# One VectorE step per decoded weight, PSUM as four two-bank tiles, and the later batches' attention form from batch 1 on

## The chip, the core and the metric

The kernel runs on one core of a Trainium2 chip. A core has a matrix engine (TensorE, PE in the profile; PEld is its weight loading), three engines that work on vectors (VectorE or DVE, ScalarE or ACT, GpSimd or POOL), and SyncE (SP), which here issues every DMA. Matrix products land in PSUM, eight banks of 512 fp32 columns on each of 128 partitions; everything else lies in SBUF or DRAM. The engines run side by side, each in its own program order, and wait for one another by semaphores that a framework places: it follows which instructions touch which tile. The metric is the device time of one execution in microseconds.

## The reference

Attention with two kinds of window over 8 batches, 8 heads, 576 positions and 64 channels, then a two-layer network on its output, whose nonlinearity is a rational function:

```python
scores = scale * np.matmul(q, k.transpose(0, 1, 3, 2))
scores = np.where(masks[None, :, :, :], scores, -1000000000.0)   # 32 last positions, or every 4th of 128
attn = np.exp(scores - max) / (sum + 1e-09)
x = np.matmul(attn, v)                                           # 4608 tokens x 512
h = x @ w_in                                                     # 512 x 2048
g = (a[0] + a[1]*h + a[2]*h2 + a[3]*h3) / (1 + |b[0]|*|h| + |b[1]|*h2 + 1e-6)
out = g @ w_out                                                  # 2048 x 512
```

The weights arrive as 64-bit floats.

## The kernel before

**Two halves of work.** The attention is cut into 48 units, six for each batch (class `Unit`, line 258): one unit is the scores of 128 rows against their windows, softmax, and the product with v. The network is cut into 144 tiles (class `Tile`, line 711): nine chunks of 512 tokens (eight batches' first 512, and one chunk `x_left` of what is left over from all batches) by 16 blocks of 128 hidden channels. One tile is 12 matmuls into `h` (line 720), the rational function on ACT, POOL and DVE (lines 773 to 788), and 12 matmuls into the four accumulators `out0` to `out3` (line 755). Every operand of the network is split into a high and a low part, so each product is three matmuls. Chunk 0's tiles run in two groups of eight with all of chunk 1 between them, and chunks 2 to 8 follow (line 943).

**The order.** A planner (class `Plan`, line 78) knows every step with its engines and an assumed duration, plays the program through, and writes the instructions down in the order in which its steps start; each engine keeps that order (`pin`). Its tables (`DUE`, `LATE`, `SLACK`, lines 31 to 34) shift the ranks of steps, and `takes` says which buffer a step needs and whose end frees it. The planner doesn't wait on the chip: it only sets the order.

**PSUM.** Two banks `h` take turns (`PS_BUFS`, line 848), four hold the accumulators, and two, `att` and `dec`, serve the attention and the decode. Each is a tile of its own until batch 3's attention starts; then `att` and `dec` become the two halves of one two-bank tile, `pair` (lines 851 to 864). From then on the halves are used by the later batches' units and, at the very end, by two tiles of the network, whose `h` goes into `att` and `dec` (line 717).

**The uses of `h`.** For each tile PE writes it with 12 matmuls; ACT reads it twice (`a<-h`, the absolute value, and `t<-h,na_t`, a line of the numerator); DVE then has `t<-t,h`, `h<-t,na_t,h`, `h<-h,na_t,r` and `a<-a,h`. Between DVE's second and third step lies a longer way by other buffers: ACT and POOL make the denominator in `a` and `r`, and ACT takes its logarithm and the exponential of the negative.

**Attention, two forms.** Batches 0 to 2 use one bank for scores, with places in halves of 64 rows; masks are added by PE in most units (`ON_PE`, line 29), and then the exponents go block by block, six instructions with their sums (`exp_bank`, line 346). PE transposes the probabilities (line 381 on), two copies put them into a zeroed tile, and PE multiplies them with v (`o_ps`). Batches 3 to 7 (`rows`) use both halves of `pair` at once in blocks of 32 rows; DVE transposes the probabilities in 32 x 32 blocks, they go to DRAM and come back in another order, PE multiplies, DVE transposes the result and it takes a second trip through DRAM. One unit is open at a time: the product with v of a unit is issued with the next one's scores (line 169).

**Decode.** A weight tile of 128 x 512 64-bit floats is fetched as words (32 such tiles, `w_fetch`), scaled by ACT (`w_scale`, from the high word), and put together by three DVE steps through the bank `dec`: shift left by 3, or in the low word's top bits, or in the sign (lines 653 to 663). A copy makes the high part (ACT or POOL) and POOL's subtraction the low part (lines 669 to 675). Staging tiles (`stage`, four of them) are shared by the decode, the trips through DRAM, and the results.

Of the kernel before, what the change touches and what calls it, by code (L numbers as in the profile page):

```python
# [11 lines left out]
I32 = mybir.dt.int32  # L12
AF = mybir.ActivationFunctionType
# [9 lines left out]
NU = 6  # L23
SPARE = "wo6"
HALF = NF // 2
BOTH, ON_ACT, ON_DVE = {"ACT": 450, "DVE": 500}, {"ACT": 450}, {"DVE": 500}


ON_PE = [[0, 0, 1, 1, 1, 1], [1, 1, 1, 1, 1, 1], [1, 0, 1, 1, 1, 1], [0, 0, 0, 0, 0, 0], [0, 0, 0, 0, 0, 0], [0, 0, 0, 0, 0, 0], [0, 0, 0, 0, 0, 0], [0, 0, 0, 0, 0, 0]]
PLACE = [(BOTH, BOTH), (ON_ACT, ON_ACT), (ON_DVE, ON_ACT), (ON_ACT, ON_DVE), (ON_ACT, ON_DVE), (ON_ACT, ON_DVE), (ON_ACT, ON_DVE), (ON_ACT, ON_DVE)]  # L30
DUE = [(13.95, 6.95), (76.77, -0.16), (93.75, -11.62), (46.1, 1.05), (120.4, 10.64), (81.33, -3.2), (120.08, -7.86), (195.87, 20.0)]

LATE = {"ab": -20.8, "ql": -91.15, "pl": 134.92, "qq": -111.7, "t1": 37.34, "t2": -29.76, "ln": 10.32, "ex": -6.24, "g0": 1.41, "g1": -62.33, "g2": 0.04, "gh": -105.34, "gl": 53.4, "out": 3.13}
SLACK = {"sc": -0.06, "qk0": 5.5, "v0": -9.17, "load": -12.74, "wi": 2.56, "wo": 1.08, "w": -12.47, "gl": 1.36, "out": 2.98}

EARLY_TILES = 36

ROWS = 3
LEFT = S - 512
NQ, NKEY, NV = 2 * 6 * 64, 2 * 224, 3 * 2 * 2 * 64  # L40
RQ, RKEY = 4 * 3 * 32, 4 * 128
LOG_SHIFT = 40
GUARD = 1.0 + 1e-6

# [33 lines left out]
class Plan:  # L78
# [21 lines left out]

    def due(self):
# [21 lines left out]
    def run(self):  # L123
# [10 lines left out]
        while ready:  # L134
            options = []
            for o in ready:
                before = list(o.deps)
                for tag, _ in o.takes:
                    bufs, groups = self.tags[tag]
                    if len(groups) >= bufs:  # L140
                        users = groups[len(groups) - bufs]
                        if any(u.end is None for u in users):
                            break
                        before += users
                else:
                    for eng, ns in o.engs.items():
                        shared = ports if o.lock or eng == "POOL" else 0.0
                        t = max([free.get(eng, 0.0), shared] + [d.after(eng) for d in before])
                        options.append((t, o, eng, ns))
# [12 lines left out]
            if o.lock or eng == "POOL":  # L162
# [16 lines left out]
def tile_attention_moe(  # L179
# [3 lines left out]
    qk_rows: bass.AP,  # L183
# [15 lines left out]

    early_banks = ExitStack()  # L200
    apart = early_banks.enter_context(tc.tile_pool(name="psum_apart", bufs=1, space=bass.MemoryType.PSUM))


# [54 lines left out]
    class Unit:  # L258
        def __init__(self, b, u):
            self.b, self.u, self.n = b, u, b * NU + u  # L260
            self.rows = b >= ROWS

        def load_qk(self):

            n = RQ + RKEY if self.rows else NQ + NKEY
            t = att.tile([P, NQ + NKEY], F32, tag="qk", name=f"qk{self.n}")[:, :n]
            load(t, qk_rows[self.n - ROWS * NU] if self.rows else qk[self.n])
            cut = RQ if self.rows else NQ
            self.q, self.k = t[:, :cut], t[:, cut:]

        def load_q(self, pool, tag):

            self.q = pool.tile([P, NQ], F32, tag=tag, name=f"q{self.n}")
            load(self.q, qk[self.n, :, :NQ])

        def load_k(self, pool, tag):
            self.k = pool.tile([P, NKEY], F32, tag=tag, name=f"k{self.n}")
            load(self.k, qk[self.n, :, NQ:])
# [5 lines left out]
        def bank(self, tag, what):  # L284
            if tag in PAIR:
                return two_banks(tag, f"{what}{self.n}", self.rows)
            return psum.tile([P, 512], F32, tag=tag, name=f"{what}{self.n}", bufs=PS_BUFS[tag])

        def scores(self, tag, masked):
            q_t = self.q.rearrange("p (h j m) -> p h j m", h=2, j=6)  # L290
            k_t = self.k.rearrange("p (h k) -> p h k", h=2)
            self.s = ps = self.bank(tag, "s_ps")
            pairs = [(h, j) for j in range(6) for h in range(2)]

            if masked:

                for j, cnt, m in self.masks():
                    mm(ps[:, 64 * j : 64 * (j + cnt)], ident_b, m, start=(j == 0), stop=False)
            for h, j in pairs if self.b else sorted(pairs):
                cols = slice(64 * j, 64 * j + 64)  # L300
                mm(ps[64 * h : 64 * h + 64, cols], q_t[:, h, j, :], k_t[:, h, 32 * j : 32 * j + 64], start=not masked, stop=not masked or j == 5)

        def scores_rows(self):
            join_banks()
            q_t = self.q.rearrange("p (g i c) -> p g i c", g=4, i=3)
            k_t = self.k.rearrange("p (g k) -> p g k", g=4)
            for i in range(3):
                for g in range(4):
                    for r in range(2):
                        half = slice(64 * r, 64 * r + 64)  # L310
                        mm(pair[0][32 * g : 32 * g + 32, r, 64 * i : 64 * i + 64], q_t[half, g, i], k_t[half, g, 32 * i : 32 * i + 64])
# [5 lines left out]
        def mask(self):  # L317
            s = self.blocks()
            for j, cnt, m in self.masks():
                if self.rows:  # L320
                    part = s[:, j // 3 : (j + cnt) // 3]
                    m = m.rearrange("p (r i) k -> p r i k", i=3)
                else:
                    part = s[:, j : j + cnt]
                tt(part, part, m, ALU.add)

        def blocks(self):
            if self.rows:
                return pair[0][:, :, :192].rearrange("p r (i k) -> p r i k", k=64)
            return self.s[:, :384].rearrange("p (j k) -> p j k", k=64)  # L330
# [6 lines left out]
        def max(self):  # L337
            self.mx, self.mx3 = self.small("mx")
            mx = self.mx.rearrange("p (r i) -> p r i", r=2) if self.rows else self.mx
            pin(nc.vector.tensor_reduce(mx, self.blocks(), axis=AX, op=ALU.max))  # L340
# [5 lines left out]
        def exp_bank(self, pool, tag):  # L346
            self.new_p(pool, tag)
            s = self.blocks()
            self.sm, self.sm3 = self.small("sm")
            for j in range(6):  # L350
                act(self.p[:, j], s[:, j], AF.Exp, bias=self.mx3[:, j // 2, j % 2 : j % 2 + 1], scale=0.125, accum_out=self.sm[:, j : j + 1])

        def new_p(self, pool, tag):
            self.p = pool.tile([P, 6, 64], F32, tag=tag, name=f"p{self.n}", bufs=2 if pool is att else 1)

        def sub(self, pool, tag):
            self.new_p(pool, tag)
            if self.rows:
                p = self.p.rearrange("p (r i) k -> p r i k", r=2)
                mx = self.mx.rearrange("p (r i) -> p r i", r=2)  # L360
                tt(p, self.blocks(), mx.unsqueeze(3).to_broadcast([P, 2, 3, 64]), ALU.subtract)
                return
            tt(self.p, self.blocks(), self.mx.unsqueeze(2).to_broadcast([P, 6, 64]), ALU.subtract)
# [15 lines left out]
        def transposes(self, tag):  # L379
            self.t = self.bank(tag, "t_ps")  # L380
# [3 lines left out]

        def turn(self):

            self.turned = work.tile([P, 512], F32, tag="stage", name=f"u{self.n}", bufs=4)[:, :384]
# [646 lines left out]
```

## Time and profile before

| | |
|---|---|
| median of 3 runs | 919.88 us (915.46 to 919.99) |
| the profiled execution | 917.92 us |
| its span, first to last instruction | 916.1 us |
| TensorE busy | 884.9 us, 7277 matmuls |
| VectorE, ScalarE, GpSimd busy | 727.1, 687.7, 506.8 us |
| DMA | 97.11 MB, mean 106 GB/s |

The page of the profile gives busy times by engine, the chain of work that ended last, and the costliest groups of instructions. A row of the timeline has the start in us, the duration, the engine, the line, the operation with the tiles that it writes and reads, and in brackets how long its engine had stood idle and what ended that. Buffer numbers are left out of names, so `h` stands for all tiles of that name. Busy TensorE means that at least one matmul is in its pipeline; matmuls overlap there. The granted clock is the share of full speed that TensorE was allowed.

### The profile page before, as it was taken

The numbers are of one execution on the slowest core, as the hardware profiler recorded it, in microseconds if no ns is written. First come the engines' busy times: TensorE is split into PE (matmuls) and PEld (weight loads), VectorE is DVE, ScalarE is ACT, GpSimd is POOL, SyncE is SP. The second block draws the span as 40 slices with busy tenths as digits, with TensorE's granted clock in tenths as the row PEclk, the third lists the DMA queues.
The fourth block names the chain that finished last, engine by engine and source line by source line (L and its number), as shares of the span: only waits on it lengthen the run. The fifth ranks groups of instructions, "written<-read, shape, count | busy, mean of one in ns | idle before, by whom it ended". The sixth has DMA issues, their size and how long they took to land.

```text
span 916.1 us, 19423 instructions
## 1 busy us (share of the span) xinstructions
PE 884.9 (97%) x7277; PEld 718.7 (78%) x7277; DVE 727.1 (79%) x1305; ACT 687.7 (75%) x1228; POOL 506.8 (55%) x469
## 2 busy tenths in 40 slices
PE   6789989999999999999999999999999999999998
PEld 5666768877788777888888888888888888888876
DVE  5899999996778787878788878888878687567656
ACT  4889988877767777777787777777777787777774
POOL 2467677864455555556555564655455545444442
PEclk9799999999999999999999999999999999999999
DMA  9734930024434333433353334333333110001001
GB/s 331 262 119 161 390 131 1 1 90 148 127 111 140 89 124 114 142 99 110 108 165 98 120 98 155 101 118 91 117 92 104 40 47 0 1 1 47 0 1 47
DMA packets 64414, 97.11 MB, mean 106 GB/s; under 512 B 22208, under 2 KB 42304, under 8 KB 64320
## 3 DMA queue, kind: packets, MB, share of 16 engines
q1 hardware_dynamic: 64320, 95.88, 31.7%
q8 instruction: 57, 0.93, 0.4%
q14 instruction: 37, 0.30, 0.1%
HBM read 73.57 MB, written 22.28 MB: 105 GB/s over the span
## 4 chain that ended last, share of the span: by engine, by line
PE 78%; DMA 8%; DVE 6%; ACT 4%; issue 1%; SPq 1%; POOL 1%; POOLq 0%; DVEq 0%; ACTq 0%
PE out L213 36%; PE h L213 36%; DMA wi_raw<-in_w_in_dram 4%; PE pair L213 4%; DVE a L222 2%; ACT r L216 1%; SPq L210 1%; DVE h L222 1%; DMA part<-os 1%; DMA v<-in_vp_dram 1%; PE o_ps L213 1%; PE s_ps L213 1%; DMA wo_raw<-in_w_out_dram 1%; POOL a L225 1%; DMA k<-in_qk_dram 1%
## 5 line engine op out<-in xcount | busy, mean ns | idle before, releaser
L213 PE MATMUL h<-xh,wi 128*128 128x512 f32 x1136 | 378.2, 394 | 6.8 <-DVE a L222 6.7
L213 PE MATMUL out<-gh,wo 128*128 128x512 f32 x1136 | 354.4, 393 | 1.1 <-DVE os L228 1.1
L225 POOL TENSOR_TENSOR a<-r,a 128x512 f32<-128x512 f32 x141 | 182.4, 1293 | 241.2 <-ACT r L216 233.4
L213 PEld LDWEIGHTS h<-xh,wi 128*128 128x128 f32 x1136 | 214.1, 188 | 58.3 <-DVE a L222 12.0
L213 PEld LDWEIGHTS out<-gh,wo 128*128 128x128 f32 x1136 | 210.3, 188 | 45.9 <-DVE os L228 1.6
L213 PE MATMUL h<-xl,wi 128*128 128x512 f32 x568 | 222.1, 391 | 0.0
L213 PE MATMUL out<-gl,wo 128*128 128x512 f32 x568 | 221.5, 390 | 0.0
L225 POOL TENSOR_TENSOR gl<-a,gh 128x512 fp32r<-128x512 f32 x141 | 184.7, 1310 | 18.9 <-ACT gh L216 17.2
L222 DVE SCALAR_TENSOR_TENSOR a<-a,r 128x512 f32<-128x512 f32 x141 | 98.7, 700 | 114.3 <-ACT r L216 113.9
L216 ACT ACTIVATE r<-a,ln_bias 128x512 f32<-128x512 f32 x141 | 101.8, 722 | 64.7 <-POOL a L225 64.4
L216 ACT ACTIVATE a<-h 128x512 f32<-128x512 f32 x140 | 84.0, 600 | 55.4 <-PE h L213 52.5
L213 PEld LDWEIGHTS out<-gl,wo 128*128 128x128 f32 x568 | 106.6, 188 | 22.9 <-POOL gl L225 0.5
L216 ACT ACTIVATE r<-a,ab_t 128x512 f32<-128x512 f32 x141 | 114.7, 814 | 13.2 <-DVE h L222 7.3
L213 PEld LDWEIGHTS h<-xl,wi 128*128 128x128 f32 x568 | 107.2, 189 | 21.1
L216 ACT ACTIVATE t<-h,na_t 128x512 f32<-128x512 f32 x142 | 109.6, 772 | 5.1 <-PE h L213 4.4
L222 DVE SCALAR_TENSOR_TENSOR h<-t,na_t,h 128x512 f32<-128x512 f32 x142 | 107.3, 755 | 4.8
L222 DVE SCALAR_TENSOR_TENSOR h<-h,na_t,r 128x512 f32<-128x512 f32 x142 | 106.4, 749 | 5.6 <-ACT r L216 4.4
L216 ACT ACTIVATE r<-r,exp_bias 128x512 f32<-128x512 f32 x144 | 104.1, 723 | 4.4
L219 DVE TENSOR_TENSOR t<-t,h 128x512 f32<-128x512 f32 x142 | 95.6, 673 | 13.3 <-ACT t L216 13.1
L216 ACT ACTIVATE gh<-a 128x512 fp32r<-128x512 f32 x135 | 84.8, 628 | 22.6 <-PE out L213 18.1
L222 DVE SCALAR_TENSOR_TENSOR a<-a,h 128x512 f32<-128x512 f32 x140 | 96.1, 686 | 4.4
L225 POOL TENSOR_TENSOR p<-p,sm 128x384 f32<-128x384 f32 x48 | 39.9, 831 | 67.2 <-DVE sm L374 46.3
(105 smaller groups left out, 732.9 us busy)
## 6 DMA issues: line engine op xcount, KB each, us to landing
v<-in_vp_dram SPq DMA_DIRECT2D x48, 384.0 KB, 3.6
qk<-in_qk_rows_dram SPq DMA_DIRECT2D x30, 448.0 KB, 4.6
out_dram<-os SPq DMA_DIRECT2D x36, 256.0 KB, 2.3
wi_raw<-in_w_in_dram SPq DMA_DIRECT2D x16, 512.0 KB, 8.7
wo_raw<-in_w_out_dram SPq DMA_DIRECT2D x16, 512.0 KB, 8.7
qk<-in_qk_dram SPq DMA_DIRECT2D x12, 608.0 KB, 4.5
turned<-u SPq DMA_DIRECT2D x30, 192.0 KB, 2.0
results<-y SPq DMA_DIRECT2D x30, 192.0 KB, 2.1
```

The lines of the kernel that those rows point to most:

```text
L210: pin(nc.sync.dma_start(dst, src))
L213: pin(nc.tensor.matmul(o, lhs, rhs, start=start, stop=stop))
L216: pin(nc.scalar.activation(o, i, func, **kw))
L219: pin(nc.vector.tensor_tensor(o, x, y, op))
L222: pin(nc.vector.scalar_tensor_tensor(o, x, s, y, op0, op1))
L225: pin(nc.gpsimd.tensor_tensor(o, x, y, op))
```

## The change

- **Decode.** ACT scales the high word with a function that has another slope for negative numbers (`Prelu`), so that the sign comes out of the same shift. A new pass on ACT or POOL (`w_low`) turns the low word into its top bits, in place. One DVE step (`w_join`) shifts and ors, with both inputs in SBUF. The high part's copy may now also go to DVE, the low part's subtraction too. A fetch follows the join of the weight six before it.
- **Attention.** Batches 1 and 2 take the form of the later ones, with masks added on PE. Batch 0 uses blocks of 32 rows in three pairs of banks; five of its six units take one exponent for the whole block. PE transposes its probabilities into an `h` bank, and one copy brings them to SBUF. Two units are open at a time in place of one.
- **PSUM.** Four two-bank tiles, `banks`, for the whole run: accumulators in the halves of 0 and 1, `h` in the halves of 2 by turns, attention in 3 (and the last tiles' `h` there, as before).
- **Leftovers** go to DRAM, `left_dram`, and are fetched for the last chunk in four parts. There are eight staging tiles in place of four. POOL's two steps of a tile may go to DVE in the first 36 tiles. The planner's tables are new.

```diff
+KIND = [0, 0, 0, 0, 1, 0]
+EARLY_TILES, BOTH_TILES = 36, 36
+DEPTH, STAGE, AHEAD, ON_PE = 2, 8, 6, 3
...
+            self.start, self.on_pe = b == 0, b < ON_PE
+            self.pair = banks[(0, 1, 3)[u % 3] if self.start else 3]
...
+        def transposes(self):
+            self.t = h_bank()
...
+        def place(self, eng):
+            self.pT = work.tile([P, 512], F32, tag="a", name=f"pT{self.n}")[:, :384]
+            copy(eng, self.pT, self.t[:, :384])
...
-    def w_shift(key):
-
-        wb[key] = b = two_banks("dec", "%s_b%d" % key, False)
-        pin(nc.vector.tensor_scalar(b.bitcast(I32), wf[key].bitcast(I32), 3, None, ALU.logical_shift_left))
-
-    def w_low(key):
-        bits = wb[key].bitcast(I32)
-        stt(bits, w_words(key)[:, :, 0], 29, bits, ALU.logical_shift_right, ALU.bitwise_or)
-
-    def w_sign(key):
-        stt(wf[key].bitcast(I32), w_words(key)[:, :, 1], -0x80000000, wb.pop(key).bitcast(I32), ALU.bitwise_and, ALU.bitwise_or)
+        pin(nc.scalar.activation(w, w_words(key)[:, :, 1].bitcast(F32), AF.Prelu, scale=2.0**-112, alpha=-(2.0**32)))
+
+    def w_low(key, eng):
+
+        low = w_words(key)[:, :, 0]
+        if eng == "ACT":
+            act(low, low.bitcast(U32), AF.Identity, bias=low_bias, scale=LOW_SCALE)
+        else:
+            pin(nc.gpsimd.tensor_scalar(low, low.bitcast(U32), LOW_SCALE, LOW_BIAS, ALU.mult, ALU.add))
+
+    def w_join(key):
+        bits = wf[key].bitcast(I32)
+        stt(bits, bits, 3, w_words(key)[:, :, 0], ALU.logical_shift_left, ALU.bitwise_or)
...
+        if len(joined) >= AHEAD:
+            f.follows.append(joined[-AHEAD])
...
-        hi = op({"ACT": 525, "POOL": 590}, 0, lambda e: w_hi(key, e), steps[-1])
-        lo = op({"POOL": 1280}, 0, lambda e: w_lo(key, e), hi)
+        hi = op({"ACT": 525, "DVE": 400, "POOL": 590}, 0, lambda e: w_hi(key, e), steps[-1], lock=True)
+        lo = op({"DVE": 602, "POOL": 1280}, 0, lambda e: w_lo(key, e), hi, lock=True)
...
-            if self.bank in PAIR:
-                ps = two_banks(self.bank, f"h{self.i}", True)
-            else:
-                ps = psum.tile([P, 512], F32, tag=self.bank, name=f"h{self.i}", bufs=PS_BUFS[self.bank])
+            ps = h_bank() if self.bank == "h" else banks[3][:, ("att", "dec").index(self.bank)]
...
-                ops[c, o] = psum.tile([P, 512], F32, tag=f"out{o}", name=f"out{c}_{o}_{ft}")
+                ops[c, o] = banks[o // 2][:, o % 2]
...
-            both = {"DVE": 602} if tail else {"POOL": 1253}
+            both = {"DVE": 602} if tail else {"DVE": 602, "POOL": 1253} if i < BOTH_TILES else {"POOL": 1253}
...
+    left_dram = dram.tile([P, NK, 512], F32, name="left")
...
+    banks = [psum.tile([P, 2, 512], F32, tag=f"banks{n}", name=f"banks{n}") for n in range(4)]
+    h_turn = []
+
+    def h_bank():
+        h_turn.append(None)
+        return banks[2][:, len(h_turn) % 2]
...
-    x_left = const.tile([P, NK, 512], F32, name="x_left")
...
+    def fetch_left(kt):
+        lefts[kt] = t = work.tile([P, 512], F32, tag="stage", name=f"left{kt}", bufs=STAGE)
+        load(t, left_dram[:, kt])
```

More of the change, by code (lines that the diff above doesn't have):

```diff
@@ L12 @@
 I32 = mybir.dt.int32
+U32 = mybir.dt.uint32
 AF = mybir.ActivationFunctionType
@@ L99, in takes, with shares @@
         o.takes.append((tag, users))
+    @staticmethod
+    def shares(o, eng):
+        return eng == "POOL" or (eng == "DVE" and o.lock)
     def due(self):
@@ L282, in load_v, with scores @@
             load(self.v, vp[self.n])
[L284 to L295, printed above, removed]
-                for j, cnt, m in self.masks():
[L298 to L306, printed above, removed]
+        def scores(self):
+            on_pe = self.on_pe
+            if on_pe:
+                for j, cnt, m in self.masks():
+                    for r in range(j // 3, (j + cnt) // 3):
+                        mm(self.pair[:, r, :192], ident_b, m[:, 3 * r - j : 3 * r - j + 3], start=True, stop=False)
             for i in range(3):
@@ new lines, in evac_lo @@
+                either(eng, self.dst(xl, cols, d), self.src(cols), self.dst(xh, cols, d), ALU.subtract)
+            if self.start and left:
+                self.o = work.tile([P, 512], F32, tag="stage", name=f"l{self.n}", bufs=STAGE)
+                for (first, cnt), _ in left:
+                    while cnt:
+                        n = min(cnt, 96 - first % 96)
+                        copy(eng, self.left((first, n)), self.src((first, n)))
+                        first, cnt = first + n, cnt - n
@@ new lines, in left, with put_left, plan @@
+        def left(self, cols):
+            first, cnt = cols
+            return self.o[:, :384].rearrange("p (h t) -> p h t", h=2)[:, :, first : first + cnt]
+        def put_left(self):
+            for cols, d in self.pieces()[1]:
+                load(left_dram[d], self.left(cols))
+        def plan(self, by, tags):
+            b, u, start = self.b, self.u, self.start
+            s_tag, self.o_tag = (f"s{u % 3}", f"o{u % 3}") if start and u % 3 < 2 else ("att", "dec")
+            (qp, qt), (vpool, self.vt) = tags if start else ((att, "qk"), (att, "v"))
+            self.by = by
+            lq = op({"SP": 430}, 0, lambda e: self.load_qk(qp, qt), dma=(RQ + RKEY) * 512)
+            self.lv = lv = op({"SP": 430}, 0, lambda e: self.load_v(vpool, self.vt), dma=NV * 512)
+            prev, clear = None, []
+            masks = [masked, identity] if self.on_pe else []
+            if len(Unit.open) >= DEPTH:
+                prev = Unit.open.pop(0)
@@ L538, in plan @@
             no = op({"POOL": 790}, 0, lambda e: self.norm(e), rc)
-            if rows:
+            if start:
+                tr = op({"PE": 500}, 0, lambda e: self.transposes(), no, identity)
+                pl = op(BOTH, 0, lambda e: self.place(e), tr)
+                plan.takes(tr, "h", 2, [pl])
+                self.placed = [pl]
+            else:
                 tr = op({"DVE": 540}, 0, lambda e: self.turn(), no)
@@ L717, in __init__ @@
             self.bank = {-1: "att", 0: "dec"}.get(self.n, "h")
-            self.r_buf = ("stage", 4) if self.late else ("r", 1)
+            self.r_buf = ("stage", STAGE) if self.late else ("r", 1)
         def h(self):
@@ L802, in plan @@
             Tile.last_out = outs
-            plan.takes(h, self.bank, PS_BUFS[self.bank], [g2])
+            plan.takes(h, self.bank, 2 if self.bank == "h" else 1, [g2])
             if not self.late:
@@ L901, in tile_attention_moe @@
     for u in range(NU):
-        start = {
-            "banks": (f"out{u % 2}", ("out2", "att")[u % 2], ("out3", "h")[u % 2]),
-            "tiles": (
-                (wpool, f"wi{15 - u}"),
-                (wpool, f"wo{9 - u // 2}" if u % 2 == 0 else f"wi{9 - u // 2}"),
-                (wpool, f"wo{15 - u}"),
-                (work, "t") if u % 3 == 2 else (att, "p"),
-            ),
-        }
+        tags = ((wpool, f"wi{15 - u}"), (wpool, f"wo{15 - u}"))
         last, step = DUE[0]
-        Unit(0, u).plan(last - (NU - 1 - u) * step, start)
+        Unit(0, u).plan(last - (NU - 1 - u) * step, tags)
     for key in keys:
```

372 lines of the change are left out of this document (150 added, 222 removed).

## The prediction

> **What bounds the kernel now.** I read the page first, then the table of busy time by stage, the chain that ended last, the groups of instructions, and last the timeline of the end, since the change lays the kernel's PSUM out anew.
>
> ```profile
> span 916.1 us, 19423 instructions
> ...
> PE 884.9 (97%) x7277; PEld 718.7 (78%) x7277; DVE 727.1 (79%) x1305; ACT 687.7 (75%) x1228; POOL 506.8 (55%) x469
> ...
> PE 78%; DMA 8%; DVE 6%; ACT 4%; issue 1%; SPq 1%; POOL 1%; POOLq 0%; DVEq 0%; ACTq 0%
> ```
>
> ```profile
> 0.00:40.00 40.00, 25.40 (x390) 22.12 (x390) 25.68 (x65) 24.60 (x92) 14.60 (x25) 0.88 0.80 292
> 40.00:140.00 100.00, 90.11 (x590) 70.22 (x587) 92.10 (x162) 86.44 (x200) 69.83 (x63) 0.98 0.55 203
> ...
> 720.00:880.00 160.00, 160.00 (x707) 132.53 (x706) 107.36 (x158) 122.30 (x184) 77.37 (x62) 1.00 0.04 16
> ```
>
> The columns after the stretch are PE, PEld, DVE, ACT and POOL busy, granted clock, DMA share, GB/s. From 40 us on TensorE is the bound: busy 90 of 100 us up to 140 us, where VectorE is as busy (decode), and without a break at the end. The chain shows the beat:
>
> ```profile
> 740.10 2.72 PE h L213 x12
> 742.82 2.72 PE out L213 x12
> ```
>
> One tile is 12 `h` and 12 `out` matmuls, 2.72 us each way: 5.44 us, and 144 tiles make 783 us. This holds only because `h` of tile i+1 runs while DVE and ACT still work on the `h` of tile i. The timeline of an ordinary pair of tiles:
>
> ```profile
> 875.78 0.76 DVE L222 SCALAR_TENSOR_TENSOR h<-t,na_t,h 128x512 f32<-128x512 f32 x1
> ...
> 875.93 0.39 PE L213 MATMUL h<-xh,wi 128*128 128x512 f32 x1
> ...
> 878.91 0.60 ACT L216 ACTIVATE a<-h 128x512 f32<-128x512 f32 x1 [0.52 <-PE h L213]
> 879.10 0.75 DVE L222 SCALAR_TENSOR_TENSOR h<-h,na_t,r 128x512 f32<-128x512 f32 x1
> ...
> 879.41 0.78 ACT L216 ACTIVATE t<-h,na_t 128x512 f32<-128x512 f32 x1
> ```
>
> PE starts the next `h` at 875.93 in the middle of DVE's step on the last one (875.78 to 876.54), and DVE's step at 879.10 overlaps ACT's at 878.91. These are two tiles of one bank each. At the end two tiles (`att`, `dec` of line 717) sit in the two halves of the one two-bank tile `pair`, and there nothing overlaps:
>
> ```profile
> 886.66 0.76 DVE L222 SCALAR_TENSOR_TENSOR pair<-t,na_t,pair 128x512 f32<-128x512 f32 x1
> ...
> 887.47 0.50 PE L213 MATMUL pair<-xh,wi 128*128 128x512 f32 x1 [0.49 <-DVE pair L222]
> ...
> 890.52 0.60 ACT L216 ACTIVATE spare_h<-pair 128x512 f32<-128x512 f32 x1 [1.26 <-PE pair L213]
> ...
> 891.15 0.76 DVE L222 SCALAR_TENSOR_TENSOR pair<-pair,na_t,r 128x512 f32<-128x512 f32 x1 [1.10 <-ACT spare_h L216]
> ...
> 891.95 0.69 DVE L222 SCALAR_TENSOR_TENSOR a<-a,pair 128x512 f32<-128x512 f32 x1
> ...
> 892.67 0.78 ACT L216 ACTIVATE t<-pair,na_t 128x512 f32<-128x512 f32 x1 [0.70 <-DVE a L222]
> ...
> 893.48 0.69 DVE L219 TENSOR_TENSOR t<-t,pair 128x512 f32<-128x512 f32 x1 [0.85 <-ACT t L216]
> ...
> 894.21 0.76 DVE L222 SCALAR_TENSOR_TENSOR pair<-t,na_t,pair 128x512 f32<-128x512 f32 x1
> ```
>
> The step at 886.66 belongs to the first tile's half, and PE's `h` into the other half waited for it. The steps at 891.15 and 891.95 are again the first tile's; the former waited 1.10 us for ACT's read of the second tile's half, and ACT's next read waited for the latter. Eight uses of either half go in single file: from `h` at 887.47 to the end of the step at 894.21, 894.97, are 7.50 us. It happens once in the kernel before, so it costs half a microsecond there.
>
> **The change, part by part.**
>
> *The banks.* All of PSUM becomes four two-bank tiles. `h` takes turns between the two halves of `banks[2]`, cut exactly as `pair` is. So I expect of all tiles what the trace shows of those two: each use of one half waits for the last use of the other. The busy time of the instructions that touch `h`, over the whole run:
>
> ```profile
> sum 916.00, PE 415.62 PEld 318.66 DVE 400.01 ACT 183.21; mean PE 59.37 PEld 45.52 DVE 57.14 ACT 26.17
> ```
>
> PE, DVE and ACT together have 998.8 us for 142 tiles, 7.03 us each; the handovers of the timeline above bring it to 7.50, and one more to PE (887.42 to 887.47) to 7.55. No order of the uses alters the sum, so the beat goes from 5.44 to about 7.5 us. The rest of a tile must fit beside it. PE's 2.72 us of `out` leave it about 2 us idle a round. The chain beside the file (over `r`, POOL, Ln and Exp) fits too: an ordinary tile had it done 3.3 us after the step that began at 875.78, at 879.10, and in the file that place comes 4.5 us after (886.66 to 891.15). What is queued behind the added waits: on PE the `out` of an older tile and the units' matmuls, on DVE and ACT the units' and the decode's steps. Those engines have room in a round of 7.5 us, but run in the order that the planner wrote for 5.44, so some steps will sit in front of one that the single file needs.
>
> *Start and end.*
>
> ```profile
> 38.32 1.91 PE s_ps L213 x25
> 40.24 3.26 PE h L213 x12
> ...
> 898.64 2.72 PE h L213 x12
> 901.36 10.89 PE out L213 x48
> ```
>
> The first `h` starts at 40.24, the last at 898.64, 17.5 us ahead of the end. Ahead of the first stands batch 0. Three of its four units with exponents by block lose them:
>
> ```profile
> L216 ACT ACTIVATE p<-s_ps,mx 128x64 f32<-128x64 f32 x90 | 26.8, 319 | 4.4 <-DVE mx L344 4.1 <-PE o_ps L213 0.2
> ...
> L656 DVE TENSOR_SCALAR wi_b<-wi_f 128x512 int32<-128x512 int32 x16 | 11.1, 693 | 2.2 <-ACT wi_f L216 1.5
> ...
> L222 DVE SCALAR_TENSOR_TENSOR wi_f<-wi_raw,wi_b 128x512 int32<-128x512 int32 x16 | 10.8, 673 | 0.2
> ...
> L237 POOL TENSOR_SCALAR wo<-wo_f 128x512 fp32r<-128x512 f32 x12 | 7.5, 621 | 4.3 <-DVE wo_f L222 4.3
> ...
> L225 POOL TENSOR_TENSOR wo<-wo_f,wo 128x512 fp32r<-128x512 f32 x16 | 24.0, 1502 | 5.5 <-ACT wo L216 4.6
> ...
> L219 DVE TENSOR_TENSOR xl<-z,xh 128x256 fp32r<-128x256 f32 x2 | 3.2, 1608 | 0.8 <-ACT xh L216 0.8
> ```
>
> Six exponents of 0.32 us become one step of the block, up to 5.8 us of ACT for three units; the batch-1 scores at 38.32 (1.91 us) need not stand there either; fewer decode steps help. Of these 7.7 us I take six, and the first `h` at 34 us; all of them and as much again of decode would give 28, none of them with more steps on DVE 42.
>
> *Decode.* Three DVE steps (the first and last are shown, 0.69 and 0.67 us) become one, so 32 weights free some 44 us of DVE if the new step costs the same. Its two inputs lie in SBUF; the old steps had one operand in PSUM. That is priced between 0.67 (the old step) and 1.6 us (the last row: two SBUF inputs, POOL busy beside it); I take 0.9, nearest to the old row. The new pass over low words, on ACT or POOL, is not in the trace: between POOL's one-input 0.62 and its two-input 1.50; I take 0.65, since it has one input. At the new beat all this costs little, for the first 24 tiles, which need the 32 weights, take 180 us. I allow 12 us.
>
> *Batches 1 and 2.*
>
> ```profile
> 88.08 0.92 PE o_ps L213 x24
> 88.99 1.14 PE s_ps L213 x26
> ...
> 458.54 1.12 PE pair L213 x73
> 459.67 2.95 PE out L213 x12
> ```
>
> An old unit takes 2.06 us of PE, and twice the 0.23 by which a stretch behind a unit is longer (2.95 for 2.72), and three transposes, put at 0.3: 2.8. A later-form unit takes 1.12 and 0.23, and masks on PE here, put at 0.3 like the transposes: 1.6. Twelve units give back 14 us of PE, but at the new beat PE has room, so this counts at nothing; without that cover the units would cost the 1.6 each. What does count is DVE: the form adds two subtract and sum steps and four transposes a unit, whose order against `h` is the planner's. For 42 units I take 1.2 us each, two DVE steps of 0.5 to 0.6 in the way, 50 us; nothing to 2.5 us each is possible.
>
> *Leftovers, staging, queues.* 40 small stores and four loads of 256 KB go onto SP's queue, DRAM round trips of 12 more units too. DMA is at 0.04 to 0.55 after 40 us, and the store of a leftover is wanted only at tile 112: nothing. Eight staging buffers in place of four, two open units in place of one, and fetches held to six ahead: a gain, if PE were the bound, of perhaps half of its 10 idle us between 40 and 140; here nothing. `out` in halves of two tiles: each of ten group ends makes a first matmul wait for two copies in place of one, 0.7 us, inside PE's room.
>
> **The sum.** First `h` at 34; 143 beats of 7.53, 1077; units 50; decode 12; from the last `h` to the end 17.5: span 1190, and 1.8 outside it (the profiled execution took 917.92), 1192 us. The profiled execution is 0.2% under the median of 919.88, so the median is not corrected.
>
> **Rivals.**
>
> *The halves go their own way* (the other side). If the waits at the end of the kernel come from something else about `pair`, which was used across both banks before while `banks[2]` never is, `h` keeps 5.44 us and PE stays the bound. Then: 6 us earlier, 14 us of units, 5 us of stalls off 916.1: 891, with 1.8 some 893 us. It decides where a beat falls under the 5.44 us that PE needs. For it: ordinary `h` tiles overlap freely. Against: the three waits above fall on halves that no instruction of those tiles shares. The Trainium skill, "PSUM — Partial Sum Buffer", section "PSUM bank collisions raise a hardware error", says that engines in different banks do not collide; by that the chip itself asks for no wait, and this rival's 893 us would stand. The trace disagrees so far as the program's waits go: they came all the same.
>
> *The clock.* PE would idle some 2 us a round.
>
> ```profile
> 32.27 0.52 PE L383 MATMUL t_ps<-ident,p 128*128 128x128 f32 x3 [1.24 <-ACT p L216]
> 34.37 0.88 PE L383 MATMUL t_ps<-ident,p 128*128 128x128 f32 x3 [1.57 <-DVE wo_T L228]
> ```
>
> ```profile
> 30.00:40.00 10.00, 7.14 (x105) 5.88 (x101) 6.72 (x20) 8.08 (x27) 5.76 (x6) 0.67 0.63 226
> ```
>
> With two pauses of 1.24 and 1.57 us close together, the granted clock of these 10 us was 0.67. If a beat's pause did that, half of the `h` stretches would run at half clock, 2.7 us longer: 143 x 0.5 x 2.7 = 193 us more, 1385 us. The pauses here are single ones between stretches of 5 us of matmuls, hence a small chance. The Trainium skill, "TensorE: Matmul & The Clock Gate", section "Part 1: The HAM clock gate", wants an idle window of about 3.4 us for a fall; by that the sum stays at 1192. The trace agrees in part only, for its fall came with two pauses of half that length.
>
> **How the numbers follow.** Forecast 0.85, own way 0.12, clock 0.03. Within the forecast: the beat is 6.85 us (982 in all, if ACT's 0.78 and DVE's 0.69 reads may overlap after all) up to 8.0; start 28 to 42; units 0 to 105 us; decode 0 to 30. The low ends together give 1030, the high ends 1340; not all go one way, so 1095 to 1300 for 0.81 of all cases, which leaves out the other two rivals. Half a percent is about what a measurement can tell from no change. Faster by more 0.12, slower 0.87, within 0.01, a miss of the first rival.
>
> **What would show it.** Right: in the changed kernel's waits, PE's `banks` matmuls wait for DVE `banks` some hundred times, DVE `banks` steps for ACT, PE busy falls to some 75%, and the late stages, free of attention, show `h` every 7.5 us. Wrong: `h` every 5.44 us at 750 us, and first `h` before 34 us. A granted clock under 1.00 in the middle would show the second rival. DVE's joins at 0.7 or at 1.6 us settle the decode's price.

## The result, and the profile after

| | before | after |
|---|---|---|
| median of 4 runs | 919.00 us (915.46 to 919.99) | 1296.96 us (1292.06 to 1299.15) |
| ratio, 95% interval | | 1.4115 (1.4058 to 1.4172) |
| profiled execution, span | 917.92, 916.1 us | 1299.15, 1297.4 us |
| first `h`, last `h` to the end of the span | 40.2, 17.7 us | 39.7, 20.7 us |
| mean from one `h` to the next (143 rounds) | 6.00 us | 8.65 us |

The changed kernel is 41% slower. Times of whole kernels are medians; one of the four runs of `h_out_tables2` further down, 995.36 us at a granted clock of 0.84 where the other three had 0.97 or 0.98, is left out. The lines of its page that answer to those of before, its stages (columns as above), and its waits (us in total, times, longest):

```profile
span 1297.4 us, 21126 instructions
...
PE 996.8 (77%) x8118; PEld 758.6 (58%) x8118; DVE 739.2 (57%) x1316; ACT 682.6 (53%) x1083; POOL 466.7 (36%) x415
...
PEclk7688888889889998989898988989898999999999
```

```profile
40.00:140.00 100.00, 72.97 (x793) 52.86 (x792) 67.28 (x131) 63.57 (x109) 44.92 (x43) 0.83 0.57 183
340.00:1040.00 700.00, 546.20 (x4680) 417.54 (x4680) 400.93 (x736) 351.25 (x551) 247.29 (x212) 0.91 0.25 77
1140.00:1260.00 120.00, 93.47 (x392) 72.52 (x393) 57.31 (x83) 67.36 (x98) 40.82 (x33) 1.00 0.03 9
```

```profile
DVE banks L219 <- PE banks L210: 216.2, 76, 5.6
ACT a L213 <- DVE banks L219: 164.8, 59, 6.1
...
PE banks L210 <- DVE t L216: 112.0, 54, 3.5
PE banks L210 <- DVE banks L219: 107.6, 58, 3.6
...
DVE banks L219 <- ACT a L213: 80.3, 43, 3.3
ACT t L213 <- DVE banks L219: 78.7, 73, 4.1
```

No engine is full in any of these stages, and the three that touch `h` wait for one another in a ring: PE for DVE 112 times, DVE for PE 76, ACT for DVE 132, DVE for ACT 43. The timeline of one undisturbed round late in the run shows the ring. All rows are on the two halves of the one tile:

```profile
1078.99 0.50 PE L210 MATMUL banks<-xh,wi 128*128 128x512 f32 x1 [1.60 <-DVE t L216]
...
1081.64 0.39 PE L210 MATMUL banks<-xh,wi 128*128 128x512 f32 x1
...
1082.07 0.76 DVE L219 SCALAR_TENSOR_TENSOR banks<-t,na_t,banks 128x512 f32<-128x512 f32 x1 [3.13 <-PE banks L210]
...
1082.86 0.78 ACT L213 ACTIVATE t<-banks,na_t 128x512 f32<-128x512 f32 x1 [1.45 <-DVE banks L219]
...
1083.54 0.59 ACT L213 ACTIVATE a<-banks 128x512 f32<-128x512 f32 x1
...
1084.16 0.76 DVE L219 SCALAR_TENSOR_TENSOR banks<-banks,na_t,r 128x512 f32<-128x512 f32 x1
...
1084.96 0.69 DVE L219 SCALAR_TENSOR_TENSOR a<-a,banks 128x512 f32<-128x512 f32 x1
...
1085.56 0.68 DVE L216 TENSOR_TENSOR t<-t,banks 128x512 f32<-128x512 f32 x1
...
1086.29 0.50 PE L210 MATMUL banks<-xh,wi 128*128 128x512 f32 x1 [1.54 <-DVE t L216]
```

The uses follow one another end to start, over both halves: `h` from 1078.99 to 1082.03, DVE from 1082.07, ACT from 1082.86, and so on to the next `h` at 1086.29, 7.30 us. Before, a round took 5.44.

### The profile page after: what moved, and what is told of

Its sections match the earlier page's. It is cut to its first block, busy times and chain, and to the rows that moved or that the text cites. A ratio compares the mean times of both kernels' runs of the same rounds, so it can differ in the third digit from the quotient of the medians.

```text
span 1297.4 us, 21126 instructions
## 1 busy us (share of the span) xinstructions
PE 996.8 (77%) x8118; PEld 758.6 (58%) x8118; DVE 739.2 (57%) x1316; ACT 682.6 (53%) x1083; POOL 466.7 (36%) x415
## 5 line engine op out<-in xcount | busy, mean ns | idle before, releaser
L210 PE MATMUL banks<-xh,wi 128*128 128x512 f32 x1152 | 456.2, 461 | 247.7 <-DVE t L216 112.0
L210 PEld LDWEIGHTS banks<-xh,wi 128*128 128x128 f32 x1152 | 254.9, 221 | 360.1 <-DVE t L216 136.1
L210 PE MATMUL banks<-gh,wo 128*128 128x512 f32 x1136 | 359.1, 397 | 8.8 <-ACT wo L213 2.9
L210 PE MATMUL banks<-xl,wi 128*128 128x512 f32 x576 | 258.4, 449 | 0.0
L210 PEld LDWEIGHTS banks<-gh,wo 128*128 128x128 f32 x1136 | 213.4, 190 | 59.5 <-ACT wo L213 4.2
L210 PE MATMUL banks<-gl,wo 128*128 128x512 f32 x568 | 221.9, 391 | 0.0
L219 DVE SCALAR_TENSOR_TENSOR banks<-t,na_t,banks 128x512 f32<-128x512 f32 x144 | 108.6, 754 | 196.0 <-PE banks L210 193.4
L219 DVE SCALAR_TENSOR_TENSOR banks<-banks,na_t,r 128x512 f32<-128x512 f32 x144 | 108.4, 753 | 120.8 <-ACT a L213 80.3
L213 ACT ACTIVATE t<-banks,na_t 128x512 f32<-128x512 f32 x144 | 111.6, 775 | 107.7 <-DVE banks L219 78.7
L210 PEld LDWEIGHTS banks<-xl,wi 128*128 128x128 f32 x576 | 128.0, 222 | 25.5 <-DVE xl L216 0.4
```

Source lines behind the costliest of these rows:

```text
L210: pin(nc.tensor.matmul(o, lhs, rhs, start=start, stop=stop))
L213: pin(nc.scalar.activation(o, i, func, **kw))
L219: pin(nc.vector.scalar_tensor_tensor(o, x, s, y, op0, op1))
```

## The experiments

Each row of this table is one kernel, timed beside the kernel before on the same chip; the first nine differ from the kernel that they start from in the edits whose main lines the diffs show, the last three in the planner's tables as well.

| kernel | starts from | us | against before (interval) |
|---|---|---|---|
| `h_apart` | after | 930.58 | 1.0131 (1.0114 to 1.0148) |
| `before_h_joined` | before | 1288.3 | 1.4029 (1.4006 to 1.4052) |
| `after_filler` | after | 1255.01 | 1.3666 (1.3635 to 1.3698) |
| `before_one_step` | before | 937.49 | 1.0200 (1.0185 to 1.0216) |
| `before_join_kept` | before | 936.73 | 1.0205 (1.0186 to 1.0223) |
| `h_out_apart` | `h_apart` | 926.75 | 1.0098 (1.0071 to 1.0125) |
| `h_out_low_pool` | `h_out_apart` | 930.12 | 1.0121 (1.0092 to 1.0150) |
| `h_apart_three` | `h_apart` | 988.83 | 1.0768 (1.0740 to 1.0796) |
| `h_apart_first` | `h_apart` | 950.16 | 1.0345 (1.0318 to 1.0372) |
| `h_out_tables` | `h_out_apart` | 925.31 | 1.0072 (1.0057 to 1.0088) |
| `h_out_tables2` | `h_out_apart` | 925.10 | 1.0073 (1.0049 to 1.0098) |
| `h_out_batch1` | `h_out_tables2` | 914.50 | 0.9960 (0.9946 to 0.9974) |

### Is it the one tile, and that alone?

`h_apart`, from the changed kernel:

```diff
-    banks = [psum.tile([P, 2, 512], F32, tag=f"banks{n}", name=f"banks{n}") for n in range(4)]
+    banks = {n: psum.tile([P, 2, 512], F32, tag=f"banks{n}", name=f"banks{n}") for n in (0, 1, 3)}
...
-        return banks[2][:, len(h_turn) % 2]
+        return psum.tile([P, 512], F32, tag="h", name=f"h{len(h_turn)}", bufs=2)
```

> The changed kernel with one edit: h (and the transposes that share its banks) lies in two tiles of one bank each, in place of the halves of one two-bank tile; every instruction and each engine's order stay. Single-file theory: the waits of PE banks for DVE go, h starts every 5.4 to 5.6 us in the late stages, granted clock near 1.00 from 60 us on, 880 to 915 us (893 was the first rival's sum). Rival theory, that the new parts cost the time (trips through DRAM of batches 1 and 2, the masks and the order of the planner's new tables, the clock by itself): still above 1150 us.

`before_h_joined`, from the kernel before:

```diff
...
-                ps = psum.tile([P, 512], F32, tag=self.bank, name=f"h{self.i}", bufs=PS_BUFS[self.bank])
+                ps = h_bank()
...
+    h_pair = psum.tile([P, 2, 512], F32, name="h_pair")
+    h_turn = []
+
+    def h_bank():
+        h_turn.append(None)
+        return h_pair[:, len(h_turn) % 2]
```

> The kernel before with one edit: h takes turns in the halves of one two-bank tile. Single-file theory: late stages h every 7.4 to 7.5 us; over all 143 rounds a mean of 8.2 to 8.8 us with the half-clock spells and the units in the way, so 1215 to 1310 us, and PE's h waits for DVE's steps on h some hundred times. If the new parts made the changed kernel slow: within 2% of 919 us.

In both, the single file's reading held: each use of one half waits for the last use of the other. With the two banks in two tiles the changed kernel takes 366 us less; with them in one tile the kernel before takes 370 more. The waits of `before_h_joined`, and from its timeline three starts of `h` late in the run:

```profile
DVE h_pair L222 <- PE h_pair L213: 226.8, 62, 6.0
ACT a L216 <- DVE h_pair L222: 198.1, 77, 6.2
...
PE h_pair L213 <- DVE t L219: 127.2, 51, 8.6
```

```profile
1161.96 0.50 PE L213 MATMUL h_pair<-xh,wi 128*128 128x512 f32 x1 [1.74 <-DVE h_pair L222]
...
1169.47 0.50 PE L213 MATMUL h_pair<-xh,wi 128*128 128x512 f32 x1 [1.74 <-DVE h_pair L222]
...
1176.98 0.50 PE L213 MATMUL h_pair<-xh,wi 128*128 128x512 f32 x1 [1.74 <-DVE h_pair L222]
```

It is the same ring at 7.51 us a round, without one of the other parts of the change. In `h_apart` PE's `h` matmuls wait for DVE 9 times, 4.2 us in all, where the changed kernel's `banks` matmuls had 112 such waits, 220 us in all, and late in the run a round is 5.44 us again:

```profile
PE h L210 <- DVE a L219: 4.2, 9, 1.9
```

```profile
804.66 0.39 PE L210 MATMUL h<-xh,wi 128*128 128x512 f32 x1
...
810.10 0.39 PE L210 MATMUL h<-xh,wi 128*128 128x512 f32 x1
```

But it came to 930.6, above the 880 to 915 that was expected of it and the 893 of the first rival: 12 us slower than before. The rest of the change is a loss by itself; the later experiments go after that.

### Why the file took 8.65 us a round and not 7.5

`after_filler`, from the changed kernel, adds work to PE where it waits:

```diff
             mm(ps, wl, self.gh, start=False, stop=False)
+            for _ in range(2 if o < 2 else 1):
+                mm(ps, zeros, self.gh, start=False, stop=False)
```

> The changed kernel, halves joined as they are, with six more matmuls a tile on TensorE: the out products get a term with a weight of zeros (two for out0 and out1, one for the others), 0.227 us each at full clock, 1.36 a tile, in the place where PE waits for h. If the half-clock spells come from PE's pauses in the file and lengthen it: pauses of 1.7 to 2.9 us shrink to 0.4 to 1.5, the spells after 120 us all but vanish (51 in all before, under 15 here), and the kernel gets 60 to 90 us faster with 14% more work on PE: 1205 to 1240 us. If the spells have another cause, or cost nothing: 1297 or more, up to 1400 with the added work at half clock.

It became 42 us faster with 864 matmuls more. Two rows of its table of busy time by stage, the middle and the late part:

```profile
340.00:1040.00 700.00, 637.66 (x5294) 496.13 (x5293) 415.83 (x753) 372.64 (x587) 262.17 (x221) 1.00 0.26 80
1140.00:1230.00 90.00, 87.01 (x369) 68.29 (x368) 42.58 (x62) 51.18 (x76) 33.20 (x26) 1.00 0.03 12
```

The granted clock went from 0.91 to 1.00 in the first, with 6 spells at half clock in place of 51 over the run. Late, PE is now busy 97% in place of 78%, and a round is 7.47 us in both: the added 1.36 us a tile lay wholly in PE's wait. The spells' theory held in kind; the gain was 42 us and not 60 to 90. It does not account for most of what a round took above 7.5, since the rounds here still have a mean of 8.30 (first `h` at 41.29, last at 1228.80). The timeline of one of 9.0 us, without a spell, in the middle of this run:

```profile
508.35 0.68 DVE L216 TENSOR_TENSOR t<-t,banks 128x512 f32<-128x512 f32 x1
...
508.95 0.56 DVE L216 TENSOR_TENSOR banks<-banks,mask_t 128x384 f32<-128x384 f32 x1
...
509.54 0.56 DVE L309 TENSOR_REDUCE mx<-banks 128x6 f32<-128x384 f32 x1
...
510.13 0.56 DVE L216 TENSOR_TENSOR p<-banks,mx 128x384 f32<-128x384 f32 x1
...
510.61 0.75 DVE L219 SCALAR_TENSOR_TENSOR banks<-t,na_t,banks 128x512 f32<-128x512 f32 x1
...
511.40 0.50 PE L210 MATMUL banks<-xh,wi 128*128 128x512 f32 x1 [0.50 <-DVE banks L219]
```

Between the file's steps at 508.35 and 510.61 DVE works off three steps of a unit, 1.7 us, and PE's next `h` waits behind them. From tile 10 to tile 112 (tiles counted from 0 in the order of time) the rounds of this run exceed 7.47 by 99.6 us together, and 35 units have their scores and products there: 2.8 us for each. It goes with the steps that DVE does besides: the 13 rounds without a spell in which DVE begins no step but the tiles' own have a mean of 7.78 us, the 58 with four or more others 8.73.

### What the decode costs by itself

`before_one_step` puts the new decode into the kernel before and lets the planner order everything anew; `before_join_kept` puts it there with every other instruction in its old place:

```diff
-        wb[key] = b = two_banks("dec", "%s_b%d" % key, False)
-        pin(nc.vector.tensor_scalar(b.bitcast(I32), wf[key].bitcast(I32), 3, None, ALU.logical_shift_left))
+        low = w_words(key)[:, :, 0]
+        pin(nc.gpsimd.tensor_scalar(low, low.bitcast(U32), LOW_SCALE, LOW_BIAS, ALU.mult, ALU.add))
...
-        stt(bits, w_words(key)[:, :, 0], 29, bits, ALU.logical_shift_right, ALU.bitwise_or)
+        pass
...
-        stt(wf[key].bitcast(I32), w_words(key)[:, :, 1], -0x80000000, wb.pop(key).bitcast(I32), ALU.bitwise_and, ALU.bitwise_or)
+        stt(bits, bits, 3, w_words(key)[:, :, 0], ALU.logical_shift_left, ALU.bitwise_or)
```

> The kernel before with the decode alone changed: scale with Prelu, a pass over the low word on ACT or POOL, one join on DVE for 32 weights; banks, tables, staging as before. DVE's busy time falls by about 2 x 0.68 x 32 = 43 us less the low passes' share on other engines; the join takes 0.68 to 0.76 us as in the changed kernel. If DVE holds up the stretch from 40 to 140 us (PE idle 10 us there), 910 to 918 us; if that idle has other causes, within 0.5% of 919; if the freed DVE time is paid back by ACT and POOL, up to 925.

> The kernel before with the decode alone changed and every other instruction in its old place: scale with Prelu where the scale stood, the pass over the low word on POOL where the shift was issued, the one join where the old third step stood; 64 VectorE steps of 0.68 us fewer, 32 passes of 0.70 on POOL more. If the decode itself is a gain and only the new order of all steps made the earlier trial 937.5: 910 to 918 us, by up to the 10 us that PE idles from 40 to 140 us. If POOL's and ACT's part of the decode holds the tiles up more than the old steps did: 920 to 935.

Both are 2% slower, though the second keeps the old order: a new order is not needed for the loss. The stage where the decode ends, before and in `before_join_kept`:

```profile
140.00:180.00 40.00, 40.00 (x176) 32.63 (x176) 38.86 (x60) 33.27 (x51) 33.39 (x28) 1.00 0.00 1
```

```profile
140.00:180.00 40.00, 36.93 (x153) 29.02 (x152) 27.20 (x38) 30.12 (x48) 35.71 (x31) 0.96 0.00 1
```

VectorE falls from 38.86 to 27.20 us of 40 and PE from 40.00 to 36.93, while POOL, which got the new passes, rises from 33.39 to 35.71. The groups of the decode in `before_join_kept`, and PE's waits for POOL from 140 to 240 us (us in total, times, longest), show what that did:

```profile
L224 DVE SCALAR_TENSOR_TENSOR wi_f<-wi_f,wi_raw 128x512 int32<-128x512 int32 x16 | 14.3, 892 | 7.6 <-POOL wi_raw L656 6.5 <-POOL wi L239 0.9 <-DMA part<-os 0.2
L224 DVE SCALAR_TENSOR_TENSOR wo_f<-wo_f,wo_raw 128x512 int32<-128x512 int32 x16 | 12.8, 799 | 16.7 <-POOL wo_raw L656 16.7
L239 POOL TENSOR_SCALAR wo<-wo_f 128x512 fp32r<-128x512 f32 x12 | 11.7, 977 | 1.0
```

```profile
PE out L215 <- POOL gl L227: 6.9, 8, 2.0
```

The joins waited 23 us for POOL's passes (6.5 and 16.7), and POOL's copy of 0.62 us before takes 0.98. POOL also makes `gl`, the low part of a tile's g, and PE waited for it 8 times, 6.9 us; the kernel before has no such wait there. At tile 24 `before_join_kept` is 17.5 us behind the kernel before, and that hardly changes up to the end (18.0): the whole loss lies where the weights are decoded. In `before_one_step` one round alone lost 12 us (18.04 us at 347), so its time is no price of the decode. The old decode in the new layout, `h_apart_three`, with three VectorE steps in SBUF:

```diff
...
-            lw = op({"ACT": 620, "POOL": 620}, 0, lambda e: w_low(key, e), f, consts)
-            jn = op({"DVE": 640}, 0, lambda e: w_join(key), sc, lw, lock=True)
+            sh = op({"DVE": 400}, 0, lambda e: w_shift(key), sc)
+            lw = op({"DVE": 640}, 0, lambda e: w_low(key), sh, lock=True)
+            sg = op({"DVE": 640}, 0, lambda e: w_sign(key), lw, lock=True)
```

> h in banks of its own, and the decode in the old three VectorE steps (in SBUF here, through the staging tile), without the pass over the low word. If the one-step decode is worth its place where VectorE is the busy engine (44 us less of it from 40 to 140 us): 8 to 25 us over 930.6. If ACT's and POOL's share of the decode holds the start up as much as VectorE did: 925 to 936.

It is 58 us slower, more than either reading. One round of 57.3 us, at 111.5, holds most of it (PE waits of 9.05, 15.77 and 9.59 us there); the planner had drawn up another order, which suits the chip worse. So this prices the order with the decode, not the decode. What can be said: put alone into the kernel before, with every pass over a low word on POOL, the new decode costs 2%. Whether it is a gain together with the other part of the change, which lets the copies and subtractions of a weight, and of the first 36 tiles, go to VectorE too, was not tried and stays open.

### Where the other 12 us of `h_apart` lie

Its tile 13 starts at 144.4 us, 11.6 later than before (132.8). That overstates what the start costs, for the kernel before has units still to do: between tiles 24 and 28 it runs four of them and `h_apart` one, and at tile 28 `h_apart` is 4.6 us behind (233.3 against 228.8). Some 6 us more are lost between tile 40 (4.1 behind) and the last `h` (10.3 behind), and none of the runs below was aimed at these. In the start the granted clock is lower too, 0.89 from 40 to 140 us where the kernel before had 0.98:

```profile
40.00:140.00 100.00, 85.45 (x877) 62.95 (x874) 83.12 (x154) 75.57 (x129) 55.32 (x50) 0.89 0.68 221
```

TensorE had 51 us at half clock in `h_apart` and 17 in the kernel before; no run separates this from the pauses that it goes with. `h_out_apart` gives each accumulator a tile of its own as well:

```diff
...
-                ops[c, o] = banks[o // 2][:, o % 2]
+                ops[c, o] = out_bank(o, f"out{c}_{o}_{ft}")
...
```

> h in banks of its own, and the four accumulators in four tiles of one bank each from the first tile on (batch 0's attention has the two pairs until then). If the joined accumulators cost about a microsecond at each of the ten group ends (the period of 16 tiles is 96.3 us with h apart, 95.4 in the kernel before): 5 to 9 us under 930.6, so 921 to 926. If the group ends are not it: 930.

926.75, 3.8 us less than `h_apart`, with intervals that overlap a little. The period of 16 tiles, from which the gain was expected, stayed 96.4 us (tiles 48 to 64, 354.9 to 451.2), so the group ends were not it, and whether anything was gained is open. The timeline of its start has a long pause of PE ahead of a product with v of batch 1:

```profile
57.18 0.96 PE L210 MATMUL banks<-v,pT 64*32 64x64 f32 x48 [6.43 <-DMA turned<-u]
```

Its probabilities were still on their way through DRAM beside the loads of the weights. `h_out_low_pool` sends all low passes to POOL (order kept), `h_apart_first` puts batch 1's scores behind batch 0's last product:

```diff
-        if eng == "ACT":
+        if False:
             act(low, low.bitcast(U32), AF.Identity, bias=low_bias, scale=LOW_SCALE)
```

```diff
+                if self.n > NU:
+                    sc.follows.append(Unit.last_av)
```

> h and accumulators in banks of their own, order of all steps kept, but every pass over a low word goes to POOL (ACT has half of them otherwise, and stands 9 us from 40 to 140 us waiting for a weight's DMA ahead of one). If these waits on ACT held the first tiles up: 3 to 6 us under 926.8. If the first tiles wait for batch 1's trips through DRAM (PE stood 6.4 us from 50.8 to 57.2 for the first unit's probabilities to come back and v), it stays within 2 us of 926.8; if POOL's own queue is the tighter one, up to 932.

> h in banks of its own, and the scores of batch 1's units from the second on come after batch 0's last product with v in the order (with h apart, PE stood 1.6 us and again inside 35.29 to 39.02 waiting for the second unit's q and k, with batch 0's last product behind it). If that order is why the first h came at 40.5 and not at 34: first h at 35 to 37, and 2 to 5 us off the 930.6. If decode or DMA is late next: first h earlier but the end within 1 us of 930.6.

The first moved nothing that can be told with certainty (930.1 against 926.8), and PE's pause in the same place was 6.4 us again, so ACT's waits don't explain it. The second missed: first `h` at 41.4, and 20 us lost, most of it in one round of 27.6 us at 98.5, again by the planner's new order. Then the planner itself was told what the traces showed, and its tables searched anew, in two searches:

```diff
-    DMA_START, DMA_NS, DMA_RATE = 3300.0, 1600.0, 400.0
+    DMA_START, DMA_NS, DMA_RATE = 3300.0, 2400.0, 400.0
...
-                sc = op({"PE": 1000 + 300 * self.on_pe}, 0, lambda e: self.scores(), lq, *masks)
+                sc = op({"PE": (1000 + 300 * self.on_pe) * (1.4 if start else 1.0)}, 0, lambda e: self.scores(), lq, *masks)
```

> h and accumulators in banks of their own, and the planner told what the traces showed of the start: batch 0's steps on TensorE 1.4 times as long (it ran them at half clock), 2.4 us for a DMA's latency in place of 1.6; its tables searched anew against those numbers, four fetches ahead in place of six. If the loss of h_out_apart (926.8, all of it before tile 13) is an order written for a full clock and quick DMAs: 905 to 918 us, faster than the kernel before, first tiles without the 6.4 us pause. If the start's work itself is longer in the new form (trips through DRAM beside the weights' loads, half clock): 920 to 930 whatever the order.

> As the other, with the tables of another search, another choice of batch 0's exponents by block and masks of batch 2 on VectorE. The same two readings: 905 to 920 if the order was at fault, 920 to 930 if the work is. Searches whose planned ends lie within 4 us should come within 8 us of each other.

925.3 and 925.1: two different orders, the same time, still slower than before, and both within the second reading. That speaks against the order, though two searches can't rule out a better one. The first has PE waiting 7.52 us for another of batch 1's trips; in the second PE's longest wait before a product with v is 1.84 us from 30 to 140 us, and it is no faster. `h_out_batch1` takes the trips of batch 1 away; the tables were searched anew for it:

```diff
-            self.start, self.on_pe = b == 0, b < ON_PE
+            self.start, self.on_pe, self.first = b <= 1, b < ON_PE, b == 0
-            self.pair = banks[(0, 1, 3)[u % 3] if self.start else 3]
+            self.pair = banks[(0, 1, 3)[u % 3] if self.first else 3]
...
-    vs = vw[:1].transpose(0, 1, 4, 5, 7, 8, 6, 2, 3, 9).reshape(NU, P, NV)
+    vs = vw[:2].transpose(0, 1, 4, 5, 7, 8, 6, 2, 3, 9).reshape(2 * NU, P, NV)
```

> As h_out_tables, but batch 1 takes batch 0's form (TensorE transposes its probabilities into an h bank, one copy, products straight from there, results split out of PSUM), so that no trip through DRAM stands beside the weights' loads in the first 130 us; tables searched anew for it. If those trips are what both table searches could not order away (PE stood 7.5 us at 43 us for one of them, tile 13 came 9 to 13 us later than in the kernel before): 908 to 918, tile 13 at 130 to 136 us. If decode and half clock hold the start whatever the form of batch 1: 920 to 928.

914.5 us, 0.4% faster than the kernel before, and 11 us faster than either of the two searches:

```profile
span 911.2 us, 21054 instructions
...
PE 878.6 (96%) x8124; PEld 713.4 (78%) x8124; DVE 715.9 (79%) x1284; ACT 681.0 (75%) x1123; POOL 488.9 (54%) x439
```

PE has 6.3 us less to do than before (884.9), but the two searches have nearly as little (880.6 and 878.8), so this is not what sets it apart from them. The gain lies in the start: tile 13 begins at 136.9, 4 us later than before but 5.0 and 8.8 earlier than in the searches, and at tile 40 it is 7.7 us ahead of the kernel before (293.4 against 301.0), where the searches are 2 behind. The edit and the new tables went in together. The two searches without the edit are the only control, and since one of them had lost its long pause for a trip and was no faster, it is not shown that the trips were what held the start.

## Why the prediction came out as it did

**The mechanism was right.** "Each use of one half waits for the last use of the other" is what the ring shows, and joining or parting the two banks, with nothing else, moves the time by 366 and 370 us. The rival of the halves that go their own way is out. By the Trainium skill, "PSUM — Partial Sum Buffer", section "PSUM bank collisions raise a hardware error", engines in different banks do not collide; `h_apart` agrees, for with the same instructions in the same order the overlap came back as soon as the tiles were two.

**The beat was right:** 7.53 forecast, 7.47 measured in late rounds (7.30 in the one shown). PE busy 77%, forecast 75%. The waits came as named: PE for DVE 112 times, DVE for ACT, ACT for DVE.

**The sum was short by 105 us**, in two terms. From the first `h` to the last are 1237.0 us. 143 rounds of 7.47 make 1068 (forecast 1077). The other 169 us were forecast as "units 50, decode 12". `after_filler` splits them: nearly without spells its 143 rounds took 1187.5, so 49.5 are the clock, and 119.5 the units, the decode and the order. The split is rough, for the added matmuls stand in the rounds with units too. In the changed kernel itself, between tile 10 and tile 112, the 49 rounds that a spell touches have a mean of 9.65 us and the other 53 one of 8.21: 1.44 for each of the 49 are 71 us for the clock there, which is rough as well, since it is the long pauses that bring the spells. The two mis-sized terms are then the clock, put at nothing in the sum, and the units. "Two DVE steps of 0.5 to 0.6 in the way", 1.2 us a unit, was about half of what it should be: the round above has three of them in the way, the mean over 35 units is 2.8 in `after_filler`, past the 2.5 that the working gave as its upper end, and 2.1 by the changed kernel's rounds without a spell (0.74 us above 7.47, for 102 rounds). In the kernel before DVE's steps for units lay beside PE's matmuls; in a single file whatever any of three engines does between two uses lengthens the round.

**The clock was the second rival's mechanism at a quarter of its price, or a little over a third** (49.5 or 71 us). It was given 0.03 as a case of its own, at 193 us; it should have been a term. That the time still fell into the range, 3 us under its upper end, is luck as far as this term goes: the range gave it no room, and it went into what the other terms left over. The reason that spoke against it, single pauses between long stretches, holds for the pure beat: in the late stages the pauses are 1.5 to 1.7 us and the clock stays at 1.00. In the middle, units lengthen the pauses to 2 to 3 us, and there it fell.

**The start was wrong by 5.7 us**: first `h` at 39.7, forecast 34. Of the time up to it PE had 21 us at half clock (from 18.4 us on); in the kernel before it was 9.6 us. The exponents saved on ACT did not make up for that; no run shows how much of the 5.7 us is the clock. From the last `h` to the end 20.7 us passed, forecast 17.5.

**The small prices:** the join took 0.68 to 0.74 us (forecast 0.9), the low pass 0.70 on POOL and 0.76 on ACT (0.65), a unit on PE 1.73 at full clock, from 75.85 to 77.58 in `h_out_apart` (1.6). These are near. "Leftovers, staging, queues: nothing", because DMA has room, was wrong already in the changed kernel, where PE stood 6.44 us ahead of a product of batch 1, put down to the load of v:

```profile
55.87 0.96 PE L210 MATMUL banks<-v,pT 64*32 64x64 f32 x48 [6.44 <-DMA v<-in_vp_dram]
```

Beside 105 us it weighs little, and with the beat back at 5.44 a pause of 6.4 us is there again. So the first rival's 893 us was too low as well, by 38 us: it took a gain of 25 us for granted, and `h_apart` has a loss of 12. Two slips of the working did no harm: 143 beats of 6.85 are 980 and not 982, and from 887.47 to 894.97 there are seven uses, not eight.

## What to carry to other kernels

Ask of every buffer that two engines share not only whether two places exist, but whether the framework sees them as two: a single rare use of the same construction (here one pair of tiles at the end of the kernel before) shows in its waits what the many uses will cost. When a beat becomes a file through several engines, price everything that these engines do besides at full length, for nothing is hidden any more. And before a step is moved off the busiest engine, look at how full the one that receives it is.

## What the runs showed of the hardware that was not expected

The granted clock falls while PE is still busy for a good part of the time. Two places of the changed kernel, in intervals of 3.41 us as the clock's record has them, each followed by the next:

```profile
984.40:987.82 3.42, 1.20 (x6) 0.66 (x4) 3.25 (x7) 1.99 (x3) 1.78 (x2) 1.00 0.32 95
987.82:994.64 6.82, 6.17 (x15) 4.82 (x16) 1.79 (x4) 2.12 (x4) 2.51 (x2) 0.50 0.37 96
```

```profile
1120.94:1124.35 3.41, 1.67 (x8) 1.07 (x7) 1.53 (x3) 2.30 (x4) 1.50 (x2) 1.00 0.00 0
1124.35:1127.77 3.42, 3.42 (x16) 2.80 (x16) 1.32 (x2) 1.73 (x3) 1.03 (x1) 1.00 0.00 0
1127.77:1131.18 3.41, 1.36 (x7) 0.78 (x5) 2.40 (x5) 2.24 (x4) 0.83 (x1) 1.00 0.00 0
1131.18:1134.59 3.41, 2.93 (x7) 2.35 (x8) 1.12 (x2) 1.44 (x2) 1.68 (x2) 0.50 0.00 0
```

After an interval in which PE was busy 1.20 of 3.42 us, or 1.36 of 3.41, the next was at half clock; after 1.67 it was not. Over the whole run, of the full-clock intervals with PE busy under 0.48 of the time 48 of 51 were followed by half clock, and of those above it 3 of 262. The 0.48 is read off this run; in `before_h_joined` the same share divides 53 of 56 from 0 of 257. A pause of 1.7 us empties half of an interval at most; one of 2.9 us empties most of it, if it falls well inside. The Trainium skill, "TensorE: Matmul & The Clock Gate", section "Part 1: The HAM clock gate", asks for an idle window of about 3.4 us; the length of the interval agrees with these records, the idleness doesn't: idle for a little over half of the interval was enough. Hence the odd result of `after_filler`, where matmuls with zeros paid for themselves.
